# A two-layer attention and MLP kernel on one core: all engine queues in another order, and the waits of an instruction sorted

## The chip, the core and the metric

The kernel runs on one core of a Trainium2 chip. A core has five engines with a queue each: TensorE (PE in the profile; its weight loads stand apart as PEld), VectorE (DVE), ScalarE (ACT), GpSimd (POOL) and SyncE (SP), which here issues every DMA. The engines run their queues in order and wait for each other on semaphores. The metric is device time in microseconds (us) of the program.

## The reference

```python
def _A_ref(x, wqkv, wo):                  # S = 2048, D = 512
    H = 32; Dh = 16; W = 256
    q, k, v = split_heads(x @ wqkv)
    scores = einsum("bhqd,bhkd->bhqk", q, k) * Dh ** -0.5
    scores = where(0 <= i - j < W, scores, -1e9)
    return merge_heads(softmax(scores) @ v) @ wo
def _B_ref(x, w1, b1, w2, b2):            # F = 1792
    return gelu(x @ w1 + b1) @ w2 + b2
x = A_x
for _ in range(2):
    x = x + _A_ref(_layernorm(x), A_wqkv, A_wo)
    x = x + _B_ref(_layernorm(x), B_w1, B_b1, B_w2, B_b2)
```

Two layers, with the same weights in both: attention in a sliding window of 256 positions with 32 heads of 16, then an MLP with gelu (tanh form). Data is bfloat16; sums in PSUM are float32.

## The kernel before

The 2048 positions are 16 tiles of 128, kept in SBUF as X throughout. Attention works on blocks of two tiles: 8 blocks in a layer, so blocks 0 to 15 over both. The MLP works on jobs of two or four tiles (`JOBS`, L483), 0 to 9.

For a block the stages are these. The layer norm takes statistics on DVE (L618, L620), adds eps (L624, on POOL or DVE), takes the power -0.5 on POOL (L630) and writes xn on DVE (L640); a DMA transpose turns xn into xnTA for attention or xnTB for the MLP (L645; the first four tiles go through PE, L652). Q, K and V are projected on PE (L666, `lnq`, `kv`), two K chunks or one 512-column matmul in a step. Q and V are copied out of PSUM by DVE or ACT (`evac`, L607 or L609), K is copied and masked by DVE (L700); two DMAs make a copy of V with its halves exchanged (L715). A visit (block, number) is a group of scores on PE (L767, one PSUM bank each for four row groups) followed by two exponentials on ACT (L774) and by masks that multiply E on DVE or POOL (L795). After five visits, twice in a block, a P.V group on PE (L819) sums the results; DVE transposes them out of PSUM (L828), takes a reciprocal (L832), DVE or POOL normalises (L836), DVE transposes back (L842). The output projection is L666 again and is added to X on DVE (L868).

An MLP job multiplies xnTB with W1 (L666), 14 groups. The first six of them get their bias on DVE (L891) and the gelu from ACT in pairs (L894), the others bias and gelu from ACT out of PSUM (L899). W2 sums over 14 steps in a PSUM bank (L666, the rows with `W_sb,gT`); DVE adds X plus b2, which POOL made (L907), and writes X (L911). The second layer's X goes out by DMA (L915). ACT needs another table for gelu than for exp; the profile shows an ACT_TABLE_LOAD at each of the 18 changes.

The code lists these steps as nodes (3078 of them) in program order, with their reads and writes. Nothing is planned at run time: `_ORDER` gives the order in which all nodes are recorded, and so each engine's queue; `_ALT` lists the nodes that run on their second engine; `_TURNS` adds pairs that share a scratch buffer, so that one waits for the other; `_BANKS` gives each PSUM group its bank. `_PV_SEQ` orders the matmuls of a P.V group. All of these lists are numbers found beforehand.

`_Sched.op` records a node. For each read and write it collects the newest producer by counter (one semaphore for each compute engine, eight in turn for SP's DMAs), drops those that the engine already knows of (`_acquire`, which also takes over all that the producer knew), and emits a wait for each that is left, then the instruction. An instruction can carry one wait. In the compiled program the first wait in the list is on the instruction, and each further one is in a separate semaphore instruction ahead of it (one of these can hold two). The lists as recorded have 1789 waits; 100 of PE's nodes have two, 35 more than two.

Of the kernel before, what the change touches and what calls it, by code (L numbers as in the profile page):

```python
# [19 lines left out]
class _Sched:  # L20
# [3 lines left out]
    COUNTERS = ("pe", "act", "dve", "pool") + tuple("spdma%d" % i for i in range(8))  # L24

    def __init__(self, nc, ctx):
        self.nc = nc
        self.prog = {e: [] for e in self.ENGINES}
        self.cnt_sem = {}
        for c in self.COUNTERS:  # L30
            self.cnt_sem[c] = ctx.enter_context(nc.semaphore("cnt_" + c))
        self.cnt_val = {c: 0 for c in self.COUNTERS}
        self.know = {e: {} for e in self.ENGINES}
        self.snap = {}
        self.res_w = {}
        self.res_r = {}
        self.seen = set()
        self.tomb = {}
        self.dma_rr = 0
        self.waitstat = {}  # L40
        self.n_extra_waits = {e: 0 for e in self.ENGINES}
        self.n_insts = {e: 0 for e in self.ENGINES}
# [19 lines left out]
    def op(self, eng, fn, reads=(), writes=(), counter=None, inc=1, dma=False):  # L62
# [39 lines left out]
        for c, v in req.items():  # L102
            if self._acquire(eng, c, v):
                waits.append((c, v))
        val = self.cnt_val[counter] + inc
        self.cnt_val[counter] = val
# [876 lines left out]
```

## Time and profile before

| | |
|---|---|
| median of 3 runs | 440.76 us (440.67 to 441.24) |
| profiled execution, device time | 440.81 us |
| its span in the profile | 439.3 us |
| PE matmul busy | 415.7 us, 95% |
| ACT busy | 386.7 us, 88% |
| DVE busy | 335.9 us, 76% |
| POOL busy | 209.1 us, 48% |
| granted TensorE clock | full in every slice |

A row of the groups reads: line, engine, operation, tile written and tiles read, shape, count, then busy time, mean in ns, and the idle time of the engine ahead of these instructions with what ended most of it. A row of the timeline has start, duration, engine, line and operation; in brackets stands the idle time ahead of it. A row by stretch has the busy time of PE, PEld, DVE, ACT and POOL with the count of instructions, then the granted clock, the share of the DMA engines and GB/s. The chain of waits is followed back from the last instruction; "issue" is time in which nothing that the profile shows was waited for.

### The profile page before, as it was taken

How to read it: one execution, taken by the hardware profiler on the slowest of the kernel's cores; microseconds unless marked ns; L12 is line 12 of the kernel's file. 1: busy time of each engine (PE TensorE's matmuls, PEld its weight loads, DVE VectorE, ACT ScalarE, POOL GpSimd, SP SyncE). 2: the span in 40 equal slices, each digit the busy share in tenths (PEclk: the TensorE clock that was granted, in tenths of full speed). 3: DMA queues.
4: the chain of work that ended last, by engine and by line, in shares of the span. 5: the costliest groups of instructions: out<-in, count | busy, mean ns of one | idle time of the engine just before them, and what ended most of it. 6: DMA issues, size and time to landing. Idle time of an engine off the chain costs nothing.

```text
span 439.3 us, 16863 instructions
## 1 busy us (share of the span) xinstructions
PE 415.7 (95%) x7497; PEld 230.2 (52%) x7571; DVE 335.9 (76%) x635; ACT 386.7 (88%) x458; POOL 209.1 (48%) x233
## 2 busy tenths in 40 slices
PE   8989999998699989999999999999999999999997
PEld 4555756645444554454454455455564554544663
DVE  5999878789867788976899687878877586655941
ACT  3999988999999899999999989998889989899533
POOL 3776262373655366731566344442443645735040
PEclk9999999999999999999999999999999999999999
DMA  8782912102200303222040111201222003003030
GB/s 245 200 199 52 223 32 52 38 13 49 56 3 13 52 4 44 34 34 44 9 92 5 25 27 28 52 1 28 51 52 50 1 16 90 14 0 76 3 107 25
DMA packets 49060, 23.51 MB, mean 54 GB/s; under 512 B 34268, under 2 KB 48988, under 8 KB 48988
## 3 DMA queue, kind: packets, MB, share of 16 engines
q1 hardware_dynamic: 48988, 22.43, 23.2%
q8 instruction: 60, 0.98, 0.9%
q14 instruction: 12, 0.10, 0.1%
HBM read 8.00 MB, written 2.10 MB: 23 GB/s over the span
## 4 chain that ended last, share of the span: by engine, by line
PE 78%; ACT 10%; DVE 4%; issue 2%; DMA 2%; POOL 1%; SPq 1%; POOLq 0%; DVEq 0%
PE ps L666 60%; ACT E L774 9%; PE ps L767 9%; PE ps L819 8%; DMA xnTB<-xn 1%; DVE OD L828 1%; POOL E L795 1%; DVE KT L700 1%; DMA X<-in_A_x_dram 1%; ACT Va L609 0%; SPq L645 0%; DVE X L911 0%; SPq L715 0%; DVE E L795 0%; PE ps L652 0%
## 5 line engine op out<-in xcount | busy, mean ns | idle before, releaser
L774 ACT ACTIVATE E<-ps 128x1024 bf16<-128x1024 f32 x300 | 284.1, 1040 | 22.9 <-PE ps L767 21.4
L795 POOL TENSOR_TENSOR E<-E,mask 128x512 bf16<-128x512 bf16 (+2 forms) x112 | 121.6, 1098 | 108.3 <-ACT E L774 45.4
L666 PE MATMUL ps<-W_sb,gT 128*128 128x512 bf16 x415 | 106.5, 380 | 3.3 <-issue 2.6
L666 PE MATMUL ps<-xnTB,W_sb 128*128 128x512 bf16 (+1 forms) x542 | 105.6, 335 | 3.2 <-issue 1.4
L666 PEld LDWEIGHTS ps<-xnTB,W_sb 128*128 128x128 bf16 x560 | 51.9, 98 | 43.7 <-issue 4.1
L666 PE MATMUL ps<-xnTA,Wqkv_sb 128*128 128x256 bf16 x512 | 70.6, 273 | 1.8 <-DVE OD L828 1.1
L767 PE MATMUL ps<-QT,KT 32*128 32x128 bf16 (+3 forms) x1920 | 60.7, 231 | 4.7 <-ACT E L774 1.8
L666 PEld LDWEIGHTS ps<-W_sb,gT 128*128 128x128 bf16 x448 | 39.4, 98 | 43.2 <-issue 3.4
L795 DVE TENSOR_TENSOR E<-E,mask 128x512 bf16<-128x512 bf16 (+2 forms) x124 | 51.2, 437 | 13.9 <-ACT E L774 6.8
L828 DVE STREAM_TRANSPOSE OD<-ps 128x1024 f32<-128x1024 f32 x32 | 40.0, 1249 | 25.3 <-PE ps L819 25.2
L666 PEld LDWEIGHTS ps<-xnTA,Wqkv_sb 128*128 128x128 bf16 x512 | 46.4, 98 | 21.7 <-issue 3.2
L767 PEld LDWEIGHTS ps<-QT,KT 32*128 32x128 bf16 x1920 | 28.5, 92 | 51.1 <-ACT E L774 30.7
L899 ACT ACTIVATE gT<-ps,b1T 128x512 bf16<-128x512 f32 (+1 forms) x80 | 43.6, 607 | 9.9 <-PE ps L666 9.7
L907 POOL TENSOR_TENSOR Xb<-X,b2all 128x512 f32<-128x512 bf16 x32 | 36.8, 1153 | 20.5 <-DVE X L911 11.5
L618 DVE BATCH_NORM_STATS2 stat<-X 128x6 f32<-128x512 bf16 x64 | 43.3, 684 | 2.7 <-DMA X<-in_A_x_dram 1.7
L819 PE MATMUL ps<-E,Va 64*17 64x256 bf16 (+3 forms) x1920 | 41.4, 230 | 3.0 <-ACT E L774 1.3
L700 DVE TENSOR_TENSOR KT<-ps,parmask 128x1024 bf16<-128x1024 f32 x32 | 38.7, 1211 | 5.4 <-PE ps L666 5.1
L819 PE MATMUL ps<-E,Vs 64*17 64x192 bf16 (+3 forms) x1920 | 42.3, 230 | 0.0
L891 DVE TENSOR_SCALAR gT<-ps,b1T 128x512 bf16<-128x512 f32 (+1 forms) x60 | 36.8, 630 | 6.1 <-PE ps L666 5.8
L836 POOL TENSOR_TENSOR Nb<-OD,Rc 128x512 bf16<-128x512 f32 x18 | 19.0, 1057 | 43.1 <-DVE Rc L832 29.0
L630 POOL TENSOR_TENSOR rstd<-rstd,mhalf 128x2 f32<-128x2 f32 (+1 forms) x33 | 24.3, 736 | 29.1 <-DVE rstd L624 27.4
L819 PEld LDWEIGHTS ps<-E,Va 64*17 64x17 bf16 x1920 | 29.3, 84 | 13.4 <-issue 7.6
(49 smaller groups left out, 359.8 us busy)
## 6 DMA issues: line engine op xcount, KB each, us to landing
Vs<-Va SPq DMA_DIRECT2D x64, 68.0 KB, 2.1
W_sb<-in_B_w_dram SPq DMA_DIRECT2D x4, 512.0 KB, 5.7
out_dram<-X SPq DMA_DIRECT2D x16, 128.0 KB, 1.9
X<-in_A_x_dram SPq DMA_DIRECT2D x3, 512.0 KB, 6.2
Wqkv_sb<-in_A_wqkv_dram SPq DMA_DIRECT2D x4, 256.0 KB, 5.1
W_sb<-in_B_w_dram SPq DMA_DIRECT2D x1, 768.0 KB
W_sb<-in_B_w_dram SPq DMA_DIRECT2D x2, 384.0 KB, 5.5
Wqkv_sb<-in_A_wqkv_dram SPq DMA_DIRECT2D x1, 512.0 KB, 6.2
```

Source lines behind the costliest of these rows:

```text
L618: add("dve", lambda e, B, t=t, k6=k6: e.bn_stats(stat6[:, k6, :], X[:, t, :]), reads=["X%d" % t], writes=["st%d" % k6], key="bs%d" % (k + j))
L630: add("pool", lambda e, B, j=j, n=n: e.tensor_tensor(out=rstd[:, k + j : k + j + n], in0=rstd[:, k + j : k + j + n], in1=mhalf[:, 0:n], op ...
L666: r = e.matmul(ps[:, B[g][0], cols], lhsT, rhs, start=st, stop=sp)
L700: add("dve", lambda e, B, g=g, i=i: e.tensor_tensor(out=KT[:, kb, 2 * i : 2 * i + 2].rearrange("p c m a q -> p a (c m) q"), in0=ps[:, B[g] ...
L767: x = e.matmul(ps[:, bk[r], o : o + n], KT[rows, kb, c, m].rearrange("p a q -> p (a q)"), QT[rows, c, q : q + n], start=True, stop=True)
L774: add("act", lambda e, B, g_=g_, gi=gi: e.activation(E[:, 2 * gi : 2 * gi + 2, e0 : e0 + 512], ps[:, B[g_][0] : B[g_][0] + 2, :], AF.Exp, ...
L795: fn = lambda e, B: e.tensor_tensor(out=Ew, in0=Ew, in1=Mw, op=ALU.mult)
L819: x = e.matmul(ps[32 * r : 32 * r + VW, B[g][par], c % 2 * 2 * P + lo : c % 2 * 2 * P + hi], V[rows, (2 * b + m // 2) % VR, c * HC + 2 * r ...
L828: add("dve", lambda e, B: e.transpose(OD[:, s].rearrange("p a c q -> p (a c q)"), ps[:, B[g][0] : B[g][0] + 2, :]), reads=["ps:" + g], wri ...
L891: add("dve", lambda e, B, g=g, fc=fc: e.tensor_scalar(out=gT[:, fc, c0 : c0 + M], in0=ps[:, B[g][0], 0:M], scalar1=b1T[:, fc : fc + 1], sc ...
L899: add("act", lambda e, B, g=g, fc=fc: e.activation(gT[:, fc, c0 : c0 + M], ps[:, B[g][0], 0:M], AF.Gelu_apprx_tanh, bias=b1T[:, fc : fc + ...
L907: add("pool", lambda e, B, t=t, xs=xs: e.tensor_tensor(out=Xb[:, xs, :], in0=X[:, t, :], in1=b2all[:], op=ALU.add), reads=["X%d" % t, "b2a ...
```

## The change

The lists of the order are replaced by others, and `_Sched.op` treats the waits in another way. `_PV_SEQ`, the nodes and the instructions stay.

```diff
+    LAG = {"pe": 3, "act": 7, "dve": 5, "pool": 7}
...
+        self.born = {}
...
         waits = []
-        for c, v in req.items():
+        for c, v in sorted(req.items(), key=lambda x: -self.born.get(x, 0)):
             if self._acquire(eng, c, v):
                 waits.append((c, v))
+        waits.sort(key=lambda x: self.born.get(x, 0) + self.LAG.get(x[0], 16))
         val = self.cnt_val[counter] + inc
+        self.born[counter, val] = len(self.born) + 1
...
 _ORDER = [
-    3, 14, 4, 0, 16, 33, 1, 18, 2, 34, 20, 37, 24, 32, 56, 36, 17, 35, 57, 25, 58, 60, 19, 61, 41, 59, 22, 62, 106,
...
 _ALT = [
-    62, 66, 69, 74, 94, 101, 108, 115, 120, 184, 191, 197, 201, 206, 210, 215, 219, 356, 363, 369, 373, 377, 378, 383,
...
+    62, 66, 69, 74, 94, 101, 108, 115, 120, 169, 191, 197, 201, 210, 215, 223, 356, 369, 373, 377, 378, 382, 383, 392,
...
 _TURNS = [
-    112, 13, 9, 156, 9, 158, 158, 10, 158, 11, 158, 12, 158, 197, 201, 205, 201, 328, 330, 206, 383, 382, 383, 223,
...
+    110, 7, 7, 112, 112, 8, 112, 9, 112, 13, 12, 156, 158, 197, 158, 369, 201, 205, 206, 210, 206, 215, 382, 388, 382,
...
 _BANKS = [
...
```

`born` numbers the nodes in the order in which they are recorded. The needed producers are now looked at from the newest to the oldest, so that an old one that a newer one implies is dropped, and those that are left are sorted by their number plus a lag for their engine. The lists then have 1742 waits, and 99 of PE's nodes have two.

What the new lists do, counted by node: of the masks (L795) 48 move from POOL to DVE and 38 from DVE to POOL; DVE has 134 of them (124 before) and POOL 102 (112). Of the normalisations (L836) 5 go to DVE and 7 to POOL. Of the copies out of PSUM (L607, L609) 8 go to DVE and 6 to ACT. DVE has 646 nodes (635), ACT 438 (440), POOL 220 (229). ACT changes between exp and gelu as often as before. The order of the score groups and of the P.V groups on PE is the same but for one pair: the scores of visit (14,1) go ahead of block 13's second P.V group. What else is moved on PE are matmuls of L666 and, at the start, warm-up matmuls (alike among themselves) and one transpose (L591). SP's first 30 DMAs are the same in the same order, later ones change places.

389 rows, old and new, of tables (_ALT, _BANKS, _ORDER, _TURNS) are left out of this document.

## The prediction

> **What bounds the kernel now.** The page comes first, for the engines' totals, then busy time by stretch, since a mean over 439 us hides where an engine runs dry.
>
> ```profile
> span 439.3 us, 16863 instructions
> ...
> PE 415.7 (95%) x7497; PEld 230.2 (52%) x7571; DVE 335.9 (76%) x635; ACT 386.7 (88%) x458; POOL 209.1 (48%) x233
> ```
>
> ```profile
> core 0: us, PE busy (x) PEld busy (x) DVE busy (x) ACT busy (x) POOL busy (x), PEclk, DMA share, GB/s
> 0.00:20.00 20.00, 18.29 (x153) 10.26 (x156) 15.29 (x34) 11.54 (x15) 9.82 (x25) 1.00 0.79 233
> 20.00:40.00 20.00, 17.57 (x439) 10.96 (x442) 18.76 (x35) 18.95 (x22) 15.08 (x17) 1.00 0.59 136
> 40.00:100.00 60.00, 57.74 (x1097) 36.84 (x1102) 48.89 (x96) 56.45 (x74) 28.27 (x33) 1.00 0.34 72
> 100.00:120.00 20.00, 15.36 (x436) 8.78 (x423) 17.82 (x33) 19.90 (x24) 8.40 (x10) 1.00 0.27 50
> 120.00:160.00 40.00, 38.46 (x712) 19.85 (x717) 28.38 (x54) 37.24 (x43) 21.01 (x22) 1.00 0.11 19
> 160.00:180.00 20.00, 17.77 (x436) 9.01 (x440) 18.19 (x36) 18.89 (x21) 11.79 (x12) 1.00 0.34 43
> 180.00:380.00 200.00, 195.49 (x3558) 103.49 (x3590) 157.12 (x291) 185.52 (x212) 96.16 (x101) 1.00 0.16 34
> 380.00:439.30 59.30, 54.96 (x727) 30.97 (x715) 31.45 (x62) 38.20 (x54) 18.54 (x18) 1.00 0.16 40
> ```
>
> PE is idle for 439.3 - 415.7 = 23.6 us: 1.7, 2.4, 2.3, 4.6, 1.5, 2.2, 4.5 and 4.3 us down the rows. Between 180 and 380 us that is 4.5 / 200 = 0.023 us per us with nothing standing out, so 0.023 is what remains when PE sets the pace, and only the excess over it can move with an order: 2.4 - 0.5 = 1.9 (20 to 40), 2.3 - 1.4 = 0.9 (40 to 100), 4.6 - 0.5 = 4.1 (100 to 120), 1.5 - 0.9 = 0.6 (120 to 160), 2.2 - 0.5 = 1.7 (160 to 180), and some 3 us at each end of the program. In the 4.1 us stretch the chain of waits names another engine:
>
> ```profile
> 100.28 1.22 DVE KT L700
> ...
> 102.32 1.94 ACT E L774 x2
> 104.26 0.49 ACT Va L609
> 104.75 0.49 ACT QT L609
> 105.24 1.88 ACT E L774 x2
> 107.12 0.49 ACT Va L609
> 107.61 12.83 ACT E L774 x14
> 120.44 0.01 issue
> 120.45 3.80 ACT E L774 x4
> ```
>
> There ACT is busy 19.90 of 20 us, back to back, and PE waits for score banks. So the kernel is bound by PE, with one long ACT run inside it (100 to 124 us) and a shorter one from 158 to 171 us.
>
> **The change, part by part.** The instructions are the same; each engine gets them in another order, and some change engine. Of the masks (L795) 48 go from POOL to DVE and 38 back, of the normalisations (L836) 5 and 7, of the copies out of PSUM (L607/L609) 8 go from ACT to DVE and 6 back. The scores and the P.V groups keep their sequence on PE, but for one pair: the scores of visit (14,1) go ahead of block 13's second P.V group, where neither stands in a hole (0). What is shuffled is the projection, MLP and output matmuls between them. PE's steady work therefore stays, and only idle time counts.
>
> *Start.* The first 30 DMAs stand in the same order, and so do PE's transposes of the first two blocks; the landing of X, the statistics and xn stay what they are. The b1 transpose (L591) leaves the place ahead of the fourth Q matmul pair, and K's first pair moves behind it:
>
> ```profile
> 11.31 0.18 PE L591 MATMUL ps<-ident,b1raw 14*128 14x14 bf16 x1
> ...
> 11.85 0.60 ACT L609 ACTIVATE QT<-ps 128x512 bf16<-128x512 f32 x1 [0.77 <-PE ps L666]
> 12.34 1.02 ACT L774 ACTIVATE E<-ps 128x1024 bf16<-128x1024 f32 x1
> ```
>
> The L591 step is worth about 0.1 us, and ACT's first exponential can start up to 0.3 us sooner. Bounds -0.3 and 0; I take -0.1, since ACT stops again before 26 us for a bank that DVE frees.
>
> *Around 53 us.* PE idles 0.62 us before the score group of visit (2,1), which waits for the last gelu before the table load:
>
> ```profile
> 53.25 1.28 ACT L774 ACT_TABLE_LOAD   x1
> ...
> 53.63 0.40 PE L767 MATMUL ps<-QT,KT 32*128 32x256 bf16 x8 [0.62 <-ACT gT L899]
> 54.54 1.02 ACT L774 ACTIVATE E<-ps 128x1024 bf16<-128x1024 f32 x1
> ...
> 83.05 1.02 PE L666 MATMUL ps<-W_sb,gT 128*128 128x512 bf16 x4 [0.18 <-issue]
> ```
>
> Afterwards five W2 matmuls stand ahead of that group and one output matmul goes behind it, four more in front. Four W2 matmuls in a row take 1.02 us at 83.05 us, the last one's tail included, so at least 0.62 us of work is there to fill the hole, and the group still ends near 54.5 us, when the table is loaded (53.25 + 1.28). Gain between 0 and 0.62; I take -0.45, as PE's pipeline restart is part of the 0.62.
>
> *The ACT runs.* The queue from 98.4 to 124.2 us has the same 26 exponentials and 3 copies before and after, and the one from 158 to 171 us the same 15 exponentials in the same order. One more copy (V of tile 11) comes to ACT just ahead of the first run, where ACT waits for the scores of visit (3,8). Both runs keep their length: 0, bounds -0.6 (start earlier) and +0.5 (the added copy, 0.49 us as the Va row above).
>
> *160 to 174 us.* PE's longest hole stays: Q of block 8 waits for the bank that DVE's transpose frees, and the order there is the same.
>
> ```profile
> 159.63 1.26 DVE OD L828
> ...
> 160.93 0.11 PEld L666 LDWEIGHTS ps<-xnTA,Wqkv_sb 128*128 128x128 bf16 x2 [1.28 <-DVE OD L828]
> ...
> 173.91 0.11 PEld L666 LDWEIGHTS ps<-xnTB,W_sb 128*128 128x128 bf16 x2 [0.75 <-DMA xnTB<-xn]
> ```
>
> Behind it DVE loses an xn and two masks, but the masks land on POOL ahead of the rstd that feeds the second wait, the one for block 5's xnTB. So -0.2, bounds -0.75 (that wait gone) and +0.5.
>
> *Wait order.* The list of waits is sorted so that the last to end stands last. In the compiled program, though, the list's first entry sits on the instruction itself and is tested last; the others become separate semaphore instructions in front. So the late wait is now mostly tested first. Two cases of before give the price:
>
> ```profile
> 83.10 1.26 DVE OD L828
> ...
> 84.40 0.12 PEld L767 LDWEIGHTS ps<-QT,KT 32*128 32x128 bf16 x8 [0.83 <-DVE OD L828]
> 156.78 1.24 DVE KT L700
> 158.12 0.12 PEld L819 LDWEIGHTS ps<-E,Va 64*17 64x17 bf16 x4 [0.37 <-issue]
> ```
>
> In the first the late wait is on the instruction: 84.40 - 84.36 = 0.04 us. In the second it is on a separate one: 158.12 - 158.02 = 0.10 us. 0.06 us for each PE stall on two waits; some 6 such stalls change sides, +0.35. Against it, keeping only the newest waits drops 47 of 1789; a wait already met costs PE nothing measurable, so this helps DVE and POOL alone. I take +0.2, bounds 0 and +0.6. (The Trainium skill, Perfetto Trace Analysis, section Identifying Dependency Chains, also says that waits on several engines may come as EventSemaphore instructions ahead of the instruction; by that every order would do, +0 instead of +0.2; the two rows above speak for a difference.)
>
> *The rest.* The other holes (1.9 + 0.9 + 0.6 us of excess) are dealt anew; with no row that says which way, 0.
>
> Sum: -0.1 - 0.45 + 0 - 0.2 + 0.2 = -0.55 us. The profiled execution took 440.81 us with its 1.5 us around the span, 0.05 over the median of 440.76; so 440.2 us.
>
> **Rivals.** *The search removes most scattered holes too.* The excess outside the start, the end and the long ACT run is 1.9 + 0.9 + 0.6 + 1.7 = 5.1 us. Half of it gone gives -2.5: 438.2 us. For it: ten masks fewer on POOL, where one is dear.
>
> ```profile
> L795 POOL TENSOR_TENSOR E<-E,mask 128x512 bf16<-128x512 bf16 (+2 forms) x112 | 121.6, 1098 | 108.3 <-ACT E L774 45.4
> L795 DVE TENSOR_TENSOR E<-E,mask 128x512 bf16<-128x512 bf16 (+2 forms) x124 | 51.2, 437 | 13.9 <-ACT E L774 6.8
> 276.64 1.06 POOL L836 TENSOR_TENSOR Nb<-OD,Rc 128x512 bf16<-128x512 f32 x1 [3.50 <-DVE Rc L832]
> 277.73 0.29 DVE L795 TENSOR_TENSOR E<-E,mask 128x256 bf16<-128x256 bf16 x1 [0.55 <-POOL Nb L836]
> ```
>
> The mask at 277.73 starts as the unrelated POOL instruction ends (276.64 + 1.06 = 277.70): these two kinds don't overlap. Each net move frees 1.098 - 0.437 = 0.66 us of time that only one of the two can have, 6.6 us in all. Against it: in the long ACT run neither is the limit. (The Trainium skill, SBUF — State Buffer, section SBUF: two separate sides, has this as an exclusive lock between GpSimd and a Vector instruction with two SBUF inputs; the rows agree.)
>
> *DVE becomes the bound (slower).* From 215 to 292.8 us DVE carries 124 instructions; the new order puts 132 between the same two P.V groups; the 8 more are mostly masks, at 0.437 us 3.5 us.
>
> ```profile
> 215.00:292.80 77.80, 76.04 (x1286) 39.74 (x1301) 64.80 (x124) 73.64 (x86) 40.76 (x42) 1.00 0.16 33
> 229.40:246.90 17.50, 17.21 (x273) 8.94 (x280) 14.47 (x27) 17.03 (x21) 12.06 (x13) 1.00 0.08 17
> ```
>
> Five of them fall in the second row (27 become 32): 14.47 + 5 x 0.437 = 16.7 of 17.5 us, 95%. The two stretches where DVE is busy 89% and 91% (17.82 and 18.19 of 20) are those where PE idles most. If a stretch like the one at 160 opens here, PE loses its 2.2 us: 442.4 us. It decides once a P.V group waits for a mask behind DVE's queue. Against it: POOL has two instructions fewer there, 2 x 1.098 = 2.2 us in which DVE's masks needn't wait for it.
>
> *The wait order does nothing or the reverse.* Counted in the sum; alone it can't exceed +0.6, 440.8 us.
>
> **How the numbers follow.** About 0.2%, 0.9 us, is what can be told from no change: below 439.9 faster, above 441.6 slower. The worked sum has 0.50, with an own range of 439.2 to 441.2 (its bounds: -1.6 and +1.0, narrowed since they won't all fall one way): 0.18 of it below 439.9, 0.31 within, 0.01 above. The scattered holes closing has 0.22, DVE as the bound 0.28. So faster 0.40, same 0.31, slower 0.29. The range goes from just under the one rival to the other: 438.0 to 442.4.
>
> **What will show it.** PE's busy sum near 415.7; the hole at 53 us gone; ACT back to back for some 25 us from 98 us, with PE idle 4 us and more from 100 to 120; the L666 wait for DVE's transpose near 161 us still above 1 us; stalls on two waits restarting 0.10 us after the later. DVE's busy share from 229 to 247 us and PE's idle time there tell of the slower rival; PE idle from 20 to 100 and 160 to 180 us falling below 4 us, of the faster. The prediction is wrong if a hole of over 1 us opens where PE now runs through (180 to 380 us), or if either ACT run shortens.

## The result, and the profile after

The changed kernel took 442.23 us (median of 15 runs, 440.24 to 444.15) beside 440.66 us before (15 runs, 439.14 to 441.35). The ratio is 1.004, with a 95% interval of 1.0028 to 1.0053: slower, where 440.2 us and "faster" had been forecast. The time lies in the range given (438.0 to 442.4), on the wrong side of the kernel before.

The loss has two parts, as every run gives its device time and its span. Outside the span lie 2.08 us (median) where it was 1.52. The span itself is 440.06 us on the mean; before, the mean device time of 440.45 less 1.52 gives 438.93. So +1.1 us is in the span and some +0.6 outside.

The page of the changed kernel begins with:

```profile
span 440.6 us, 16837 instructions
...
PE 416.7 (95%) x7500; PEld 230.3 (52%) x7571; DVE 337.7 (77%) x646; ACT 386.1 (88%) x456; POOL 197.1 (45%) x224
```

By stretch, with the same cuts as before:

```profile
core 0: us, PE busy (x) PEld busy (x) DVE busy (x) ACT busy (x) POOL busy (x), PEclk, DMA share, GB/s
0.00:20.00 20.00, 17.81 (x164) 10.16 (x170) 15.93 (x37) 12.42 (x16) 10.48 (x25) 1.00 0.81 237
20.00:40.00 20.00, 18.36 (x449) 11.26 (x448) 18.51 (x33) 18.87 (x22) 13.36 (x17) 1.00 0.58 132
40.00:100.00 60.00, 57.69 (x1082) 36.24 (x1090) 50.58 (x102) 56.38 (x74) 23.36 (x27) 1.00 0.32 70
100.00:120.00 20.00, 14.29 (x407) 8.64 (x408) 16.89 (x30) 19.60 (x23) 7.64 (x9) 1.00 0.34 53
120.00:160.00 40.00, 39.06 (x581) 19.10 (x587) 27.73 (x54) 35.35 (x41) 19.66 (x22) 0.96 0.10 20
160.00:180.00 20.00, 17.25 (x553) 9.70 (x560) 17.37 (x31) 18.51 (x21) 13.75 (x14) 1.00 0.23 30
180.00:380.00 200.00, 195.58 (x3505) 102.96 (x3536) 157.29 (x297) 185.43 (x211) 91.21 (x97) 1.00 0.18 37
```

From 180 to 380 us PE is as busy as before (195.58, 195.49). PE gains 0.8 us between 20 and 40 us (18.36, was 17.57). It loses 1.1 us between 100 and 120 (14.29, was 15.36), and the next row is the only one with a clock below 1.00. There the chain of waits, which named ACT's exponentials from 107 to 124 us before, now names a DMA:

```profile
106.33 0.61 issue
107.33 1.49 PE ps L668 x8
108.84 0.70 DVE X L870
109.56 0.69 DVE stat L620
110.27 0.70 DVE X L870
111.00 0.70 DVE stat L620
111.97 1.11 DVE KT L702
113.68 1.19 SPq L647
115.41 4.36 DMA xnTB<-xn
120.12 1.33 PE ps L668 x3
```

This is the transpose of the last tile (11, layer 1) for MLP job 2. It takes 4.36 us from issue to landing, and PE waits for it. The timeline of PE (start, duration, engine, line and operation, idle time ahead in brackets), first before, then after:

```profile
117.75 0.40 PE L767 MATMUL ps<-QT,KT 32*128 32x192 bf16 x12 [0.26 <-ACT E L774]
118.97 0.81 PE L666 MATMUL ps<-xnTB,W_sb 128*128 128x512 bf16 x3 [0.82 <-ACT E L774]
```

```profile
117.72 0.40 PE L769 MATMUL ps<-QT,KT 32*128 32x192 bf16 x12 [0.34 <-ACT E L776]
120.12 1.33 PE L668 MATMUL ps<-xnTB,W_sb 128*128 128x512 bf16 x3 [2.00 <-DMA xnTB<-xn]
121.39 0.61 PE L769 MATMUL ps<-QT,KT 32*128 32x128 bf16 x24
121.93 2.10 PE L668 MATMUL ps<-xnTB,W_sb 128*128 128x512 bf16 x5
```

The hole grew from 0.82 to 2.00 us, and behind it the same matmuls run at half speed: five take 2.10 us. The busy times over three pieces of 3.41 us, which is how long the clock stayed down, show it:

```profile
116.85:120.26 3.41, 1.08 (x68) 0.83 (x53) 2.24 (x3) 3.41 (x4) 2.23 (x2) 1.00 0.23 50
120.26:123.68 3.42, 3.42 (x32) 1.19 (x30) 1.42 (x3) 1.78 (x3) 1.81 (x3) 0.50 0.02 5
123.68:127.09 3.41, 3.26 (x28) 1.23 (x27) 3.02 (x7) 2.34 (x4) 0.72 (x1) 1.00 0.00 0
```

What the place costs is read between the P.V. groups on both sides of it, which hold the same 198 matmuls in both kernels, first before, then after:

```profile
115.99:124.93 8.94, 7.58 (x198) 3.75 (x200) 5.87 (x10) 8.43 (x10) 6.48 (x7) 1.00 0.19 42
115.93:127.19 11.26, 8.78 (x198) 4.17 (x200) 6.78 (x13) 8.55 (x10) 4.86 (x5) 0.85 0.10 21
```

It is 2.3 us: 1.1 us more of idle time (2.48 instead of 1.36) and 1.2 us more of busy time by the clock. The profiled spans differ by 440.6 - 439.3 = 1.3, so the rest of the program gave back 1.0 us, all of it behind this place: by the starts of the P.V. groups the changed kernel was 1.0 us ahead at 36 us, but only 0.1 us at 116.

The half clock doesn't come in every run. The mean clock of a run was 0.999 or 1.000 in 6 of the 15 runs, whose mean span is 439.37 us, and 0.994 to 0.996 in the other 9, with 440.52. Of another 120 runs of the kernel before, one was below 0.999.

### The profile page after: what moved, and what is told of

Its sections match the earlier page's. It is cut to its first block, busy times and chain, and to the rows that moved or that the text cites. A ratio compares the mean times of both kernels' runs of the same rounds, so it can differ in the third digit from the quotient of the medians.

```text
span 440.6 us, 16837 instructions
## 1 busy us (share of the span) xinstructions
PE 416.7 (95%) x7500; PEld 230.3 (52%) x7571; DVE 337.7 (77%) x646; ACT 386.1 (88%) x456; POOL 197.1 (45%) x224
## 4 chain that ended last, share of the span: by engine, by line
PE 76%; ACT 10%; DVE 6%; DMA 3%; issue 2%; POOL 1%; SPq 0%; DVEq 0%
PE ps L668 59%; PE ps L769 9%; ACT E L776 9%; PE ps L821 8%; DMA xnTB<-xn 2%; DVE KT L702 2%; DVE stat L620 2%; DMA xnTA<-xn 1%; ACT gT L901 1%; DVE xn L642 1%; POOL Xb L909 1%; DMA X<-in_A_x_dram 0%; DVE E L797 0%; DVE X L870 0%; DVE X L913 0%
## 5 line engine op out<-in xcount | busy, mean ns | idle before, releaser
L797 POOL TENSOR_TENSOR E<-E,mask 128x512 bf16<-128x512 bf16 (+2 forms) x102 | 108.9, 1082 | 123.9 <-ACT E L776 64.4
L668 PE MATMUL ps<-W_sb,gT 128*128 128x512 bf16 x415 | 108.1, 380 | 3.6 <-issue 2.7
L668 PE MATMUL ps<-xnTB,W_sb 128*128 128x512 bf16 (+1 forms) x543 | 106.7, 338 | 4.9 <-DMA xnTB<-xn 2.6
L668 PE MATMUL ps<-xnTA,Wqkv_sb 128*128 128x256 bf16 x512 | 71.6, 273 | 2.4 <-DVE OD L830 1.0
L797 DVE TENSOR_TENSOR E<-E,mask 128x512 bf16<-128x512 bf16 (+2 forms) x134 | 54.7, 438 | 15.1 <-ACT E L776 4.6
L821 PE MATMUL ps<-E,Va 64*17 64x64 bf16 (+3 forms) x1920 | 41.1, 230 | 1.3 <-ACT E L776 0.8
L913 DVE TENSOR_TENSOR X<-Xb,ps 128x512 bf16<-128x512 f32 x32 | 21.6, 681 | 19.5 <-PE ps L668 19.4
L668 PE MATMUL ps<-Wo_sb,OT 128*128 128x512 bf16 x120 | 33.6, 380 | 0.5 <-issue 0.5
```

The source lines that it names most:

```text
L668: r = e.matmul(ps[:, B[g][0], cols], lhsT, rhs, start=st, stop=sp)
L797: fn = lambda e, B: e.tensor_tensor(out=Ew, in0=Ew, in1=Mw, op=ALU.mult)
L821: x = e.matmul(ps[32 * r : 32 * r + VW, B[g][par], c % 2 * 2 * P + lo : c % 2 * 2 * P + hi], V[rows, (2 * b + m // 2) % VR, c * HC + 2 * r ...
L913: add("dve", lambda e, B, g=g, t=t, xs=xs: e.tensor_tensor(out=X[:, t, :], in0=Xb[:, xs, :], in1=ps[:, B[g][0], :], op=ALU.add), reads=["X ...
```

## The experiments

All times are beside the kernel before on the same chip. "Outside" is the median of device time less span. "Clock down" counts the runs with a mean clock below 0.999. It is a rough count, since in the profiles the clock also falls behind PE's last matmul, where it costs nothing, and that alone can bring the mean down to 0.998 (`sp3_dve10`).

| kernel | runs | ratio (95%) | mean span | outside | clock down |
|---|---|---|---|---|---|
| before | 120 | 1 | 439.3 to 439.6 | 1.52 | 1 |
| changed | 15 | 1.0040 (1.0028 to 1.0053) | 440.06 | 2.08 | 9 |
| hole | 12 | 1.0023 (1.0000 to 1.0045) | 440.12 | 2.11 | 6 |
| pad8 | 12 | 1.0035 (1.0015 to 1.0055) | 440.58 | 2.10 | 5 |
| before_new_waits | 12 | 1.0009 (0.9987 to 1.0031) | 439.59 | 1.75 | 1 |
| after_old_waits | 12 | 1.0008 (0.9991 to 1.0026) | 439.70 | 1.88 | 4 |
| sp3 | 12 | 0.9994 (0.9979 to 1.0009) | 438.31 | 2.12 | 1 |
| sp3_dve10 | 12 | 1.0014 (0.9998 to 1.0031) | 439.64 | 1.85 | 5 |
| after_late_on_instr | 12 | 0.9975 (0.9955 to 0.9994) | 438.00 | 2.06 | 3 |
| before_late_on_instr | 11 | 0.9958 (0.9943 to 0.9973) | 437.23 | 1.74 | 0 |
| late_on_instr_sp3 | 5 | 0.9952 (0.9937 to 0.9968) | 436.68 | 2.03 | 0 |
| before_late_pool_only | 12 | 1.0027 (1.0008 to 1.0046) | 439.85 | 1.84 | 1 |
| before_late_pe_only | 5 | 0.9962 (0.9950 to 0.9974) | 437.22 | 1.75 | 0 |
| before_late_rest_only | 12 | 1.0011 (0.9992 to 1.0030) | 439.38 | 1.73 | 1 |
| pe_late_to_58us | 12 | 0.9979 (0.9961 to 0.9997) | 437.86 | 1.88 | 0 |
| pe_late_from_58us | 12 | 0.9992 (0.9977 to 1.0006) | 438.64 | 1.72 | 0 |
| after_late_pe_only | 12 | 0.9984 (0.9969 to 0.9998) | 438.09 | 2.06 | 3 |

### The scores moved into the hole

```diff
 _ORDER: ... ex4_8_0,
+  sc4_9,
   m2_5.0, m2_5.1, m2_5.2, m2_5.3, ...
-  sc4_9,
 (_BANKS: its entries in the same order)
```

> The changed kernel with the scores of visit (4,9) ahead of the four matmuls m2_5 (the first of MLP job 2) instead of behind them. In the changed kernel PE stood still for 2.00 us before m2_5, and the granted clock was 0.5 for 3.41 us from 120.26 us on. Theory A (one hole makes the loss): the scores can run at about 119.55 us, when the exponential before them has ended (119.51), so that the hole is cut to some 1.4 us; the clock stays 1.00, which gives back 7 steps x 0.21 = 1.5 us, and 0.3 us of the hole: span 438.8, about 1.6 us less than the changed kernel (ratio to the kernel before near 1.000). Theory B (the loss is spread over the wait order and the new places): the same time as the changed kernel within 0.5 us, ratio 1.003 to 1.004. If the clock halves all the same, the length of the hole isn't what sets it.

Measured: 1.0023, with the clock down in 6 of 12 runs. The scores start at 118.73 us instead of 121.39, and yet the clock halves in the profiled run:

```profile
118.73 0.69 PE L745 MATMUL ps<-QT,KT 32*128 32x128 bf16 x24 [1.52 <-ACT E L752]
```

```profile
116.82:120.23 3.41, 1.63 (x39) 0.95 (x41) 2.10 (x3) 3.41 (x4) 2.15 (x3) 1.00 0.09 20
120.23:123.64 3.41, 2.99 (x14) 0.57 (x12) 1.85 (x4) 1.20 (x2) 1.06 (x2) 0.50 0.02 5
```

So theory A fell as it was put, and theory B, which had 1.003 to 1.004, is neither shown nor excluded by an interval of 1.0000 to 1.0045. The scores waited for ACT themselves (1.52 us), and the hole, though shorter, was still enough: the piece ahead of the fall had PE busy 1.63 of 3.41 us. The transpose landed late again, 4.3 us after its issue.

### Eight instructions more on PE

```diff
+        def warm(e, bk, n):
+            for _ in range(n):
+                e.matmul(ps[:, bk, 0:64], gT[:, 0, 0:P], gT[:, 0, 0:64], start=True, stop=True)
+            return e.matmul(ps[:, bk, :], gT[:, 0, 0:P], gT[:, 0, :], start=True, stop=True)
...
-            add("pe", lambda e, B, bk=h % 8: e.matmul(...
+            add("pe", lambda e, B, bk=h % 8, n=4 * (h == 15): warm(e, bk, n),
```

> The changed kernel with four small matmuls of 64 columns more among the warm-ups, in PE's wait for the first xn, so eight PE instructions more (15311 instead of 15303; the kernel before has 15309). Between span and device time lay 1.51 us before and 2.04 us after; the last 16 KB code packet of PE came at 431.91 us before, and at 441.65 us after, behind the end of the span. Theory A: the program's end has slid over a border between two blocks of 256 PE instructions, and the end waits for that block; eight more bring the last packet back to about 432 us and the time outside the span to 1.5 us, with the span as in the changed kernel: -0.5 us, ratio about 1.003. Theory B: what lies outside the span has to do with something else (the order on SP, the waits of the end): it stays at 2.0 us.

Measured: PE's last code packet came back to 433.3 us as expected, and the time outside stayed at 2.10 us. So where that packet stands doesn't set the time outside; theory A fell here too. The hole and the half clock were there in the profiled run (tile 11's transpose landed at 119.90 us).

### The two parts of the change alone

```diff
 # before_new_waits: before's lists, and in _Sched
+    LAG = {"pe": 3, "act": 7, "dve": 5, "pool": 7}
-        for c, v in req.items():
+        for c, v in sorted(req.items(), key=lambda x: -self.born.get(x, 0)):
+        waits.sort(key=lambda x: self.born.get(x, 0) + self.LAG.get(x[0], 16))
+        self.born[counter, val] = len(self.born) + 1
```

> The lists of the kernel before with the changed handling of the waits (newest producer first, sorted by number plus lag). It has 15303 PE instructions, as many as the changed kernel. Theory A (code blocks): 2.0 us outside the span, +0.5 us; the span within 0.3 us of that before: 439.0 to 439.6 in the profile, ratio 1.001 to 1.002. Theory B (the order of waits costs, as the prediction has it): +0.2 to +0.6 us in the span too, ratio 1.002 to 1.0025. Theory C (neither): ratio 1.000.

> The lists of the changed kernel with the handling of the waits of before (15307 PE instructions). Theory A (the places of the lists make the loss): the hole before m2_5 is there as long as one of the 16 parts of the last xnTB transpose lands late beside a 16 KB code packet of PE; ratio 1.002 to 1.004. Theory B (the wait order makes most of the loss): span 0.5 us and more under that of the changed kernel all over, with the hole still there, ratio 1.001 or less. The time outside the span is 1.5 or 2.0 us and narrows down where the border between the blocks lies (between 15303 and 15309).

Measured: 1.0009 for the new waits on the old lists and 1.0008 for the old waits on the new lists, both with intervals that hold 1. Neither part alone has a loss that can be told from none. Together they would be 1.0017, where the whole change had 1.0040 in other runs; with intervals of 0.002 each way it stays open whether the parts add up. The time outside is 1.75 and 1.88 us, between the 1.52 of before and the 2.08 of the changed kernel, so each part adds to it. With the old waits the new lists have the late landing and a hole of 2.22 us too, and in the profiled run the clock stayed at 1.00. There the hole fell on a border of the clock's pieces, which lay at 118.41 us there (33 pieces of 3.413 us after the clock came up at 5.78 us):

```profile
119.32 0.81 PE L667 MATMUL ps<-xnTB,W_sb 128*128 128x512 bf16 x3 [2.22 <-DMA xnTB<-xn]
```

```profile
115.00:118.41 3.41, 1.80 (x140) 1.48 (x140) 1.92 (x3) 3.41 (x5) 1.45 (x2) 1.00 0.31 64
118.41:121.83 3.42, 2.33 (x32) 1.01 (x33) 1.66 (x4) 2.28 (x4) 2.60 (x3) 1.00 0.02 5
```

Beside each other: the clock fell after pieces with PE busy 1.08, 1.23, 1.23, 1.25 and 1.63 us (five profiled runs), and not after 1.80, 2.15 or 2.35. The closest piece on the other side is one of the old lists with the late wait on the instruction, with 1.66 us:

```profile
51.98:55.39 3.41, 1.66 (x19) 1.01 (x18) 1.56 (x6) 2.63 (x4) 1.76 (x3) 1.00 0.19 60
```

Where these pieces begin differs from run to run: the clock came up at 4.21, 5.78 and 7.15 us in three profiled runs. That would explain why one and the same kernel has the fall in 9 runs of 15. The Trainium skill, TensorE: Matmul & The Clock Gate, section What's actually happening, says that the gate watches a free-running window of 4096 cycles at 1.2 GHz, 3413 ns; the records agree, the clock was down for 3.413 us and its changes lie 116.05 us apart, 34 such windows.

### Why the transpose lands late: three waits more on SP

```diff
+    EXTRA = {"sp": (50, 53, 56,)}
...
+        if self.n_insts[eng] in self.EXTRA.get(eng, ()):
+            waits.append(("act" if eng == "pe" else "pe", 1))
```

> The changed kernel with three waits more on SP, all long met (PE's counter at 1 or more), on three copies of V between 68 and 92 us: SP has 200 instructions instead of 197, and what follows stands three places later in its code. In the changed kernel SP stood still for 0.46 us (114.87 to 115.33) between the two transposes of xnTB for tiles 10 and 11 of layer 1, its 81st instruction, and a code packet for SP followed 0.63 us later; the same stop of 0.45 us stood in another place before (107.51 to 107.96, ahead of a copy of V). Theory A: the stop is the border between two blocks of SP's code, and moves to where SP waits anyway (about 109 us); the second transpose is issued at 114.95 instead of 115.40, and all its 16 parts land by 117.5, ahead of PE's code packet (117.77), instead of 119.77. The hole before m2_5 falls from 2.00 us to under 1.0, the clock stays 1.00 in all runs; span 437.9 to 438.6, ratio 0.997 to 0.999. Theory B (the late landing has nothing to do with SP's code or PE's packet): hole 1.8 us or more, ratio 1.002 to 1.004.

Measured: the hole and the half clock went, as theory A had it. In the changed kernel's timeline SP issues the second transpose at 115.41; with the three waits both go out back to back (2.51 us for the two) and land at 115.58 and 116.91:

```profile
115.41 1.23 SPq L647 DMA_TRANSPOSE xnTB<-xn  x1
```

```profile
113.18 2.51 SPq L650 DMA_TRANSPOSE xnTB<-xn  x2
```

```profile
118.41 0.81 PE L671 MATMUL ps<-xnTB,W_sb 128*128 128x512 bf16 x3 [0.78 <-issue]
```

The hole is 0.78 us, the clock was down in 1 of 12 runs instead of 9 of 15, and the mean span is 438.31 us beside 439.38 before: 1.1 us shorter, where the changed kernel's was 1.1 us longer. The 2.1 us outside leave a ratio of 0.9994. So the new lists seem worth about -1.1 us in the span, and the one place took about 2.2, which is what the profiles show there (2.3; with the three waits the same 198 matmuls take 9.00 us).

What made the landing late is in the landings of the 16 parts into which such a DMA is split. In the changed kernel 15 of tile 11's had landed at 117.88 us and the last at 119.77; meanwhile a code packet of PE was under way (16 KB, 117.77 to 118.72). Before, a packet at about the same time (117.16 to 118.63) met two copies of V, whose last parts landed 1.55 and 1.09 us after the others, and nobody waited for them. Over the profiled runs of all 17 kernels here, from 60 us on, 335 of 1950 DMAs had a last part 0.6 us or more behind the 15th; beside 323 of these a code packet of PE was under way, while of the 1078 DMAs without one only 12 were late. So a late part is far more common with a packet beside the DMA (323 of 872) than without, but not certain.

Why this transpose is caught in one kernel and not in another is open. The last part of tile 11's landed late in 6 of the 17 profiles, each time 1.0 to 1.2 us after the end of the packet. In the changed kernel the packet began 0.11 us ahead of the 15th landing (117.88). In before it began 0.12 us ahead of it (117.16, 117.28) and with the three waits 0.03 us (116.88, 116.91), and there no part of this transpose was late. So the three waits hardly moved the transpose against PE's packet. They also took away SP's own stop ahead of the transpose and an 8 KB code packet beside it (115.96 to 116.45). Whether that packet has a part in it no run tells; with the old waits the transpose, issued at 114.47 us, was late though such a packet was over at 114.17.

### The time outside the span

```diff
+    EXTRA = {"sp": (50, 53, 56,), "dve": (333, 342, 356, 366, 400, 417, 426, 435, 470, 477,)}
```

> As the kernel with three waits more on SP, and ten waits more, long met, on DVE between 200 and 372 us (707 instructions instead of 697). The time outside the span was 1.53 us before, 1.75 for before's lists with the new waits, 1.88 for the changed lists with the old waits, 2.08 for the changed kernel, while the number of PE instructions didn't move it. Theory A: what is outside the span is the end of the program on SP and DVE crossing a border of their code: SP's lies near its 208th instruction and DVE's near its 704th; with DVE past it before the end, the time outside falls to about 1.75 us, and the span is that of the kernel with three waits more on SP (each DVE wait costs 0.03 us, off the path). Theory B: it stays near that of the kernel with three waits more on SP alone, and the cause lies elsewhere.

Measured: 1.85 us outside instead of 2.12, so DVE's number of instructions has a part in it: 2.03 to 2.12 us in all kernels with 697, 1.72 to 1.88 with 674 or with 705 and 707. The number alone doesn't order them: before has 683 and 1.52 us. Of that difference 0.2 is accounted for otherwise: there SP's last semaphore instruction starts 0.22 us after those of the other engines (439.27, 439.05), inside the span, and in the changed kernel with them (440.52, 440.53). That both are code borders fits (code packets were seen 0.6 us after the end in before, 1.1 us after it with the old waits), but is not shown. The span was 1.3 us longer than with SP's three waits alone. In the two profiles (438.9 and 437.4 us) 0.7 us of that had gathered by PE's last matmul, which ended at 435.11 and 434.43 us, more than ten waits of 0.03 us; why is open. The other 0.8 us lie behind it: the last two DMAs of the output had their last parts 1.2 and 0.8 us behind the 15th, beside an 8 KB code packet (436.74 to 437.08) that isn't there with SP's waits alone. So in the profiled run more came back inside the span than was saved outside it.

### The late wait on the instruction

```diff
-        waits.sort(key=lambda x: self.born.get(x, 0) + self.LAG.get(x[0], 16))
+        waits.sort(key=lambda x: self.born.get(x, 0) + self.LAG.get(x[0], 16), reverse=True)
```

> The changed kernel with the waits sorted the other way, so that the one whose producer ends last stands first in the list and is on the instruction itself; the same number of instructions on every engine. Theory A (the prediction's price of the wait order): some six PE stalls restart 0.06 us sooner and POOL's and DVE's likewise: the span is 0.2 to 0.6 us shorter than in the changed kernel, the time outside unchanged (2.06): ratio 1.002 to 1.0035. Theory B (the price is lost in waits elsewhere): same as the changed kernel, ratio 1.004. The hole before m2_5 stays in both.

> The lists of the kernel before, the newest producer first, and the waits sorted with the late one on the instruction. Against before's lists with the waits sorted as in the change (same span as before, 0.22 us more outside it, ratio 1.0009) theory A gives 0.2 to 0.4 us less: ratio 0.9995 to 1.0005; theory B the same ratio, 1.0005 to 1.0015. The time outside the span stays at 1.75 us if it depends on the number of instructions of SP and DVE alone.

Measured: 0.9975 for the new lists and 0.9958 for the old ones, far more than either theory gave. The span falls from 439.59 to 437.23 us on the old lists and from 440.06 to 438.00 on the new ones (the 440.06 from other runs, beside another before). The number of instructions is the same on each engine, only which wait stands on the instruction is changed. Both edits together:

> The changed kernel with both edits that helped: the late wait on the instruction, and three waits more on SP ahead of the last xnTB transposes. Each alone had a mean span of 438.0 and 438.3 us beside 439.4 before. Theory A (two separate causes, the wait order everywhere and the hole at 118 us): the gains add, span 436.2 to 437.0, some 2.06 us outside, ratio 0.994 to 0.996. Theory B (both did the same thing, the late landing avoided): span 437.5 to 438.3, ratio 0.997 to 0.999.

Measured: 436.68 us and 0.9952, in the range of theory A. Counted from the changed kernel, whose span was 1.1 us above before, the edits alone gave 2.2 and 2.5 us and both together 3.8, so the gains add for the most part. Its median of 438.83 us and the 439.26 us of the old lists with the late wait on the instruction are 2.0 and 1.4 us under before; between the two nothing can be told.

### Which engine it is

```diff
-        waits.sort(key=..., )
+        waits.sort(key=..., reverse=eng in ('pool',))            # before_late_pool_only
+        waits.sort(key=..., reverse=eng in ('pe',))              # before_late_pe_only, after_late_pe_only
+        waits.sort(key=..., reverse=eng in ('dve', 'sp', 'act')) # before_late_rest_only
```

> The lists of before with the changed handling of the waits, and the order turned round on POOL alone (late wait on the instruction); the other engines as in the change. Turned round on all engines the span was 437.2 us on the mean beside 439.4, and as in the change 439.6. Theory A (POOL's restarts are what costs: 25 stalls of before have the late wait on a separate instruction and take 0.133 us each, 3 do so with the order turned round, 0.068 us): most of the gain is here, span 437.3 to 438.0, ratio 0.996 to 0.998. Theory B (PE's restarts): span as before, ratio 1.000 to 1.001.

> As the kernel with the order turned round on POOL alone, but on PE alone. Theory A (POOL): ratio 1.000 to 1.001. Theory B (PE): span 437.3 to 438.0, ratio 0.996 to 0.998. Counted from the trace PE has only two to four stalls with a late wait on a separate instruction, 0.06 us each: 0.25 us at most.

> As the kernel with the order turned round on POOL alone, but on DVE, SP and ACT alone. Theory A (POOL) and theory B (PE): ratio 1.000 to 1.001. Theory C (DVE or SP: a transpose's wait for xn stands on a separate instruction and SP takes 0.1 instead of 0.04 us; six DVE stalls of 0.093 instead of 0.023 us): span 437.3 to 438.5, ratio 0.996 to 0.999.

Measured: 1.0027, 0.9962 and 1.0011. PE alone carries it (theory B); POOL, where in before most of the late waits on separate instructions stand, gives nothing and perhaps a loss. Counted in the profiles over stalls of more than 0.1 us, PE has the late wait on a separate instruction 12 times with the waits as in the change on the old lists, and 4 times with PE's order turned round. Eight times 0.06 us is 0.5 us, not 2.

```diff
+        waits.sort(key=..., reverse=eng == "pe" and self.n_insts["pe"] < 195)   # pe_late_to_58us
+        waits.sort(key=..., reverse=eng == "pe" and self.n_insts["pe"] >= 195)  # pe_late_from_58us
```

> The lists of before with the changed handling of the waits, and on PE, for its first 195 nodes alone (up to 57.6 us), the late wait on the instruction. Turned round for all of PE the span was 437.2 us on the mean beside 439.3. Theory A (the gain lies where transposes and loads land late, in the first 55 us: the two profiles differ by 1.4 us at 54 us and by 1.7 at the end): most of it is here, span 437.4 to 438.0, ratio 0.9965 to 0.998. Theory B (each restart on PE, all over the program): 0.3 us at most, ratio 0.999 to 1.001.

> The other half: the late wait on the instruction from PE's 196th node on (after 57.6 us). Theory A: 0.3 us less at most, ratio 0.9995 to 1.001. Theory B: span 437.5 to 438.2, ratio 0.997 to 0.9985.

> The changed kernel with the late wait on the instruction on PE alone. On all engines it had a span of 438.0 us on the mean (437.5 with the clock at 1.00) beside 439.4, and 2.06 us outside. If PE's order alone carries it here too, span 437.5 to 438.3, ratio 0.997 to 0.9985; if POOL's or SP's order has a part on these lists (18 POOL stalls with a late wait on a separate instruction), 438.5 to 439.5, ratio 0.9995 to 1.002.

Measured: 437.86 us (0.9979) with the first 58 us turned round, 438.64 (0.9992, not told from none) with the rest, 438.09 (0.9984) on the new lists. Against 439.39 before, two thirds of the gain (1.5 us) lie in the first 58 us, and together the halves (1.5 + 0.75) make about the whole of 2.1; each has an interval of 0.6 to 0.8 us either way. The profiles of PE's order turned round (`before_late_pe_only`) and not turned round (`before_new_waits`), from 40 to 55 us:

```profile
40.00:55.00 15.00, 14.42 (x257) 10.08 (x257) 13.02 (x27) 14.66 (x24) 3.92 (x6) 1.00 0.81 177
```

```profile
40.00:55.00 15.00, 13.83 (x255) 9.88 (x255) 12.60 (x26) 14.53 (x22) 3.98 (x6) 1.00 0.80 180
```

The second has 0.6 us more idle time there (and 0.5 us more before 40 us). Most of it is a projection of block 4, which waits for a transpose whose last part landed at 52.33, 1.6 us after the 15th, beside a code packet (50.03 to 51.12):

```profile
52.47 0.82 PE L670 MATMUL ps<-xnTA,Wqkv_sb 128*128 128x256 bf16 x6 [0.50 <-DMA xnTA<-xn]
```

It looks like the hole at 118 us in another place, where the DMA engines are busy with loads (0.80). Whether the order of PE's waits acts through the times of such meetings, or in a way of its own, one profiled run of each kernel can't tell; that stays open.

## Why the prediction was wrong, point by point

*The ACT runs* (the 100 to 120 us stretch) are the step that failed. It took the hole ahead of job 2's first matmuls as part of an ACT run that keeps its length, and priced it at 0 between -0.6 and +0.5. It didn't ask what was late next, and no bound held a landing or the clock. There the second transpose of xnTB went out at 115.41 us (114.80 before), its last part landed late beside a code packet, and PE waited 2.00 instead of 0.82 us; with that the clock could fall. The place measured +2.3 us in the profile. The sign that the prediction itself had named came with it, since the run of exponentials did not keep its length: it went on to 124.24 us before (107.48 + 16.76), and in the changed kernel ACT stopped at 120.42 us and waited for PE's scores.

```profile
106.30 14.12 ACT L776 ACTIVATE E<-ps 128x1024 bf16<-128x1024 f32 x15
122.05 1.94 ACT L776 ACTIVATE E<-ps 128x1024 bf16<-128x1024 f32 x2 [1.64 <-PE ps L769]
```

The slower rival had its price right by chance (442.4 us) and its place wrong: DVE between 229 and 247 us. With the same P.V. groups as limits the row there is

```profile
231.40:248.90 17.50, 17.24 (x263) 8.83 (x265) 16.12 (x33) 16.97 (x21) 7.01 (x10) 1.00 0.09 20
```

DVE is busy 16.12 of 17.50 us (14.47 before, 16.7 forecast), and PE 17.24 (17.21). That rival didn't happen. One of its arguments was also misread: 20 to 40 us, where DVE was busy 18.76 of 20 us and PE idle 2.4, is left out of the stretches in which DVE is fullest and PE idles most.

*The time around the span* was taken as it was, 1.5 us. It grew by 0.55 us, a third of the loss, and no step of the sum looked at the end of the program. What makes it up is shown only in part (`sp3_dve10`).

*The start* was right in sign and too small: the first exponential starts at 11.42 us instead of 12.34, 0.9 us sooner where 0.3 was the bound, though PE's hole ahead of its first transposes differs from run to run as well. The 1.0 us by which the changed kernel led at 36 us was gone by 116 us.

*Around 53 us* was right in its mechanism. The scores of visit (2,1) have no idle time ahead of them any more, though between the P.V. groups at 49 and 68 us only 0.2 of the 0.45 us was gained:

```profile
53.14 0.82 PE L668 MATMUL ps<-xnTA,Wqkv_sb 128*128 128x256 bf16 x6
53.89 0.40 PE L769 MATMUL ps<-QT,KT 32*128 32x256 bf16 x8
```

*160 to 174 us*: that the first hole stays was right, that 0.2 us would go was not; the wait for xnTB is still there (0.85 us ahead of the weight load, was 0.75; its row says issue, but xnTB had landed only at 175.97).

```profile
162.82 0.11 PEld L668 LDWEIGHTS ps<-xnTA,Wqkv_sb 128*128 128x128 bf16 x2 [1.24 <-DVE OD L830]
...
176.07 0.13 PEld L668 LDWEIGHTS ps<-xnTB,W_sb 128*128 128x128 bf16 x2 [0.85 <-issue]
```

*Wait order*: +0.2 us (0 to 0.6) can't be told from what the part alone gave (1.0009, of which 0.2 us is the end of the program; its span was that of before). The reading that the late wait comes off the instruction was right, and turning it round pays. But the price was worked out from restarts, 0.06 us each, and the runs show 2.1 us for PE, several times its upper bound. The term leaves out something that the restarts don't contain, and what that is stays open.

*The rest* at 0 and the faster rival (half the scattered holes close): with the late landing out of the way the span was 1.1 us shorter. The forecast of -0.55 us erred towards too little gain there, and what made the sign wrong was one place and the end of the program.

*The sums*: the bounds of the terms add up to -2.3 and +1.6 us, 438.5 to 442.4 us from the time before. The worked sum's own range is narrower by choice, but its -1.6 and +1.0 give 439.2 and 441.2 only when they are counted from different times (440.76 and 440.2), and it left out the 442.23 that came. The wait order alone at its upper bound would give 440.6 us, not 440.8, since +0.2 of it is in the sum already.

## What to carry to other kernels

A landing that comes 1.7 us before it is needed (117.28 and 118.97 us in before) is no safe cover: look at what would be last next, DMA landings above all, and at where the code packets of the busiest engine fall beside them. A PE hole of 2 us can cost as much again by the clock, in some runs and not in others, so read the clock of every run before a difference of 1 us is put down to an order. And compare device time less span: an edit that changes little but how many instructions an engine has moved it by 0.3 us here, the whole change by 0.55.

## What the runs showed of the hardware that was not expected

- PE's code comes in packets of 16 KB, 59 or 60 in a profiled run, and one can hold up one of the 16 parts of a DMA beside it: 323 of 335 late last parts had a packet beside them, 0.6 us to 2.2 us each. PE itself seems to wait for its code too. In the changed kernel a score group stopped after its first matmuls at 106.07 and went on at 106.93 without any wait in the code, 1.28 us after the packet of 104.47 had ended (105.65); in before it went on at 383.08, 1.27 us after the packet that ended at 381.81; the count of PE's instructions, a matmul for each weight load, stands at the same place there, 194 and 193 modulo 256. The Trainium skill, Runtime: NRT & Kernel Launch, section Instruction fetch mechanics, gives blocks of 16 KiB, 256 instructions, and calls their cost mostly hidden; the size agrees, and here it was not hidden.
- SP stops for 0.45 us at one place of its code: in 12 of the 17 profiles 0.44 to 0.46 us lie between its 79th and 80th instruction there, whatever these are (in the other five it waits longer), so three instructions more put the stop at another place of the work.
- The clock fell after 3.41 us pieces in which PE was busy 1.63 us or less, and not after 1.66 us or more, in 16 profiles with records of the clock, so some idle time in the piece is enough; no empty piece is needed.
- Which of several waits stands on a PE instruction is worth 2 us of 439, though the stalls that change sides (eight, 0.06 us each) explain a quarter of it at most.
